# Batch 0's heads loaded together at the start, and its token weights converted behind its softmax

## The chip, the cores and the metric

The kernel runs on one NeuronCore of one Trainium2 chip. The metric is device time in microseconds (us) of one execution. Five engines run side by side, each through its own queue in order: TensorE (PE in the profile; PEld is its weight load), VectorE (DVE), ScalarE (ACT), GpSimd (POOL), and SyncE (SP), which here issues all DMAs.

## The reference

Three layers run one after the other on 4 batches of 576 positions and 512 features: a windowed attention with 8 heads, a phase-mixing layer, and a gated layer. All is float32; the weight matrices come in as float64.

```python
scores = where(mask, q @ k.T / sqrt(64), -1e9)          # window 32; heads 4..7 dilated by 4
x = softmax(scores) @ v                                  # -> (4, 576, 512)
theta = x @ w_theta
y = w_tok_r @ (x * cos(theta)) + w_tok_i @ (x * sin(theta))
u = x + y
x = u + relu(u @ w_ch)
h = relu(x @ w_in); u, v = halves(h)
out = (u * (w_spatial @ layernorm(v) + b_spatial)) @ w_out
```

## The kernel before, in words

Float32 products are made of three matmuls on rounded parts: each operand is split into a high part (`_h`) and the rest (`_l`), and high x high, low x high, high x low are summed in PSUM. Every float64 weight therefore goes through a conversion first (`split_weight`, which calls `bits64`): a DMA brings 256 or 288 columns as 64-bit words into a staging buffer `w` (tag w64, three of them); POOL or ACT scales the high words (L129 or L127, output `w64g`); DVE glues the low bits on in three instructions (L130, L131, L132, called a **triple** below); then the high part is copied out (L108 on ACT, L110 on DVE, L112 on POOL) and the low part subtracted (L143). For theta (`wth_h`, `wth_l`, 8 pieces) all but the triple is on POOL. The token weights `wtok_h`, `wtok_l` are 9 row blocks in two column halves of 9 pieces each: **tok0** (scale and high part on ACT, low part on POOL) and **tok1** (scale and high part on POOL, low part on DVE). `w_ch` has 8 pieces.

The stages of batch 0 are: attention, in 12 groups (4 head pairs hp, 3 groups g each): scores `s` (L220) and masks (L213) on PE, the maximum on DVE (L227), three exponentials on ACT (L235), sum and reciprocal on DVE (L236, L237), the product on POOL (L238), transposes (`pt`, L247), a copy (`pT`, L249), values (`ps_x`, L261 and L265) and copies to `x` (L268 to L277). Then theta in five units (`th_unit`): DVE splits x (`xh`, `xl`, L316, L317), PE forms `ps_th` (L322), ACT and DVE make sine and cosine, and `zh`, `zl` come out (L110, L112, L297). Then the token mixing `tm_run`: `ps_y` (L377) takes 9 row blocks times 3 matmuls for each of 8 outputs, added to x on DVE (L380). Then `ch_run` (`ps_r`, L395) with `w_ch`. Batch 1's attention is woven into the mixing of batch 0 and so on.

A call of `spread(main, (fill, rate), ...)` writes the program in the order main step, then `rate` steps of each fill. A scheduler then orders each engine's queue from that, and the queues run in that order on the chip: an instruction that waits holds all behind it on its engine. `tc.issue_after(i)` puts what is written under it behind instruction i in i's own queue. Buffers: head pairs alternate between two places for q (`qzero`), k and v, so head pair 2 can be loaded only when head pair 0's scores are done.

Of the kernel before, what the change touches and what calls it, by code (L numbers as in the profile page):

```python
# [2 lines left out]

# [19 lines left out]
DM = H * D  # L23
# [16 lines left out]


LAG_T, LAG_V = 2, 4
W_RATE0 = 0.75
ATT_RATE, ATT_RATE_PAIR = 2.0, 3.0
TAIL_RATE = 1.0
CH_BEFORE = 4
# [15 lines left out]
def tile_block(ctx: ExitStack, tc: tile.TileContext, qT, kT, vw, eye_in, mask_in, eye_b_in, w_theta, w_tok, w_ch, w_in, w_sp, w_sph, b_sp, w_out, out):  # L62
# [43 lines left out]
    def copy(dst, src, eng):  # L106
# [4 lines left out]
        else:  # L111
            G.tensor_scalar(dst, src, 1.0, 1.0, op0=ALU.mult, op1=ALU.mult)  # L112

    def bits64(src, n, eng):

        p = src.shape[0]
        st = const.tile([P, 2 * CH], U32, tag="w64", name="w64", bufs=3)
        SY.dma_start(st[:p, :2 * n], src.bitcast(U32))  # L120
        w = st[:p, :2 * n].rearrange("p (n w) -> p n w", w=2)
        lw, hw = w[:, :, 0], w[:, :, 1]
        g = const.tile([P, CH], F32, tag="stage", name="w64g", bufs=4)[:p, :n]
        c = c64[:p, :n].bitcast(U32)
        gi = g.bitcast(U32)
        if eng == "a":
            A.mul(g, hw.bitcast(F32), 2.0**-112)  # L127
        else:
            G.tensor_scalar(g, hw.bitcast(F32), 2.0**-56, 2.0**-56, op0=ALU.mult, op1=ALU.mult)  # L129
        V.tensor_scalar(c, lw, 29, None, op0=ALU.logical_shift_right)  # L130
        V.scalar_tensor_tensor(c, gi, 3, c, op0=ALU.logical_shift_left, op1=ALU.bitwise_or)  # L131
        V.scalar_tensor_tensor(gi, gi, 0x80000000, c, op0=ALU.bitwise_and, op1=ALU.bitwise_or)  # L132
        return g
# [27 lines left out]
    def w_tok_job(k, c):  # L161
        cs = slice(CH * c, CH * (c + 1))
        split_weight(w_tok[:, k, cs], wtok_h[:, k, cs], wtok_l[:, k, cs], *TOK_ENG[c])

    def w_ch_job(k):
        halves(w_ch, wch_h, wch_l, k, DM, CH_ENG)


    x = {}
# [3 lines left out]
    for i, qz in enumerate(qzero):  # L173
        for j in range(2):
            (V, G)[j].memset(qz[D * (1 - j):D * (2 - j), j], 0.0)

    groups = [(b, hp, g) for b in range(B) for hp in range(4) for g in range(3)]
    att = {}
    heads = {}

    def att_load(b, hp):
        qz = qzero[(4 * b + hp) % 2]
        kt = patt.tile([P, S + WIN], F32, tag="k", name="kt", bufs=2)
        first = b == 0 and hp == 0
# [12 lines left out]
        SY.dma_start(vt, vw[b, hp])
        heads[b, hp] = (qz, kt, vt, {})

    def att_scores(m):  # L200

        b, hp, g = groups[m]
        if g == 0:
            att_load(b, hp)
        if hp == 0 and g == 0:
            x[b] = p1.tile([P, 4, S], F32, tag="x", name=f"x{b}", bufs=2)
        qz, kt, vt, pT = heads[b, hp]
        s = ps_mm.tile([P, 512], F32, tag="mm", name="s")
# [12 lines left out]
        mask_half(False)
        sm = patt.tile([P, 3, KW], F32, tag="sm", name="sm", bufs=5)
        m_ = patt.tile([P, 3], F32, tag="m", name="m", bufs=3)
        l = patt.tile([P, 3], F32, tag="l", name="l", bufs=3)
        sv = s[:, :3 * KW].rearrange("p (t k) -> p t k", t=3)
        if on_pe:
            V.tensor_reduce(m_, sv, op=ALU.max, axis=AX.X, negate=True)  # L227
            A.mul(m_, m_, D**-0.5)
            src, scale = sv, D**-0.5
        else:  # L230
            V.scalar_tensor_tensor(sm, sv, D**-0.5, masks[:, kind], op0=ALU.mult, op1=ALU.add)  # L231
            V.tensor_reduce(m_, sm, op=ALU.max, axis=AX.X, negate=True)  # L232
            src, scale = sm, 1.0
        for t in range(3):
            A.activation(sm[:, t, :], src[:, t, :], AF.Exp, bias=m_[:, t:t + 1], scale=scale, accum_out=l[:, t:t + 1])  # L235
        V.tensor_scalar_add(l, l, 1e-9)  # L236
        V.reciprocal(l, l)  # L237
        G.tensor_tensor(sm, sm, l.unsqueeze(2).to_broadcast([P, 3, KW]), op=ALU.mult)  # L238
        att[m] = sm

    def att_transpose(m):
# [117 lines left out]
    def th_run(b, ts):  # L359
        for t in ts:  # L360
            th_unit(b, t)
            yield

    def tm_run(b, ks, last=True):

        if last:
            uh = p1.tile([P, 4, S], F32R, tag="uh", name="uh")
            ul = p1.tile([P, 4, S], F32R, tag="ul", name="ul")
            uu[b] = (uh, ul)
        for c in range(2):  # L370
            cs = slice(CH * c, CH * (c + 1))
            for d in range(4):
                ps = ps_mm.tile([P, 512], F32, tag="mm", name="ps_y")
                n = 0
                for k in ks:
                    for lh, rh in ((zh, wtok_h), (zl, wtok_h), (zh, wtok_l)):
                        PE.matmul(ps[:, :CH], lh[b, k][:, P * d:P * (d + 1)], rh[:, k, cs], start=(n == 0), stop=(n == 3 * len(ks) - 1))  # L377
                        n += 1
# [63 lines left out]
    j_out = [lambda k=k, c=c: stored(w_out, wo_d, k, slice(H2 * c, H2 * (c + 1)), OUT_ENG) for k in range(4) for c in range(2)]  # L442

    second = jobs(j_in + j_sp + j_out)
    spread(attention(0), (jobs(j_theta + j_tok0), W_RATE0))
    spread(th_run(0, (4, 0, 1, 2, 3)), (jobs(j_tok1), 1.0))
    for b in range(PAIR):
        ch = ch_run(b)
        spread(chain(tm_run(b, K_ALL), take(ch, CH_BEFORE)), (attention(b + 1), ATT_RATE), (take(second, 12) if b else jobs(j_ch), 1.0 if b else 0.5))
        run(th_run(b + 1, (4, 0, 1, 2, 3) if b + 1 < PAIR else (0, 1, 2, 3)))  # L450
        run(ch)

# [300 lines left out]
```

## Time and profile before

| | |
|---|---|
| runs | 575.29, 578.91 and 1181.34 us; median 578.91 |
| profiled execution | 575.99 us, of which the profile's span is 574.2 us |
| PE busy | 538.3 us (94% of the span) |
| DVE, ACT, POOL busy | 329.7, 243.3, 259.6 us |
| PE granted clock | 0.97 of full in the mean; below 0.9 only in some slices of the first 80 us and one later |

Engine shares are means over stages; the change lies in the first quarter of the span, so stretches of that quarter have to be read by themselves. Times in rows are microseconds from the span's start unless marked ns.

### The profile page before, as it was taken

To read this page: it belongs to the slowest core of one execution; us is meant where nothing else is said; L and a number is where in the kernel's file an instruction comes from. 1 tells how busy PE (TensorE), PEld (TensorE's weight loads), DVE (VectorE), ACT (ScalarE), POOL (GpSimd) and SP (SyncE) were. 2 spreads that over 40 slices of the span, in tenths; PEclk is the share of its full clock that TensorE was granted. 3 is DMA by queue.
4 is the path that set the end of the run, shared out by engine and by line. 5 is a ranking of instruction groups with operands and counts; after the bars stand their busy time and mean duration, and the time that the engine had idled before them with its cause. 6 is when DMAs were issued, how large, how long until landed. Compare 5 with 4: busy or idle time off the path is not lost.

```text
span 574.2 us, 11260 instructions
## 1 busy us (share of the span) xinstructions
PE 538.3 (94%) x4148; PEld 479.7 (84%) x4148; DVE 329.7 (57%) x842; ACT 243.3 (42%) x712; POOL 259.6 (45%) x329
## 2 busy tenths in 40 slices
PE   4958889999999999999799999999999999999997
PEld 2745668888988798888688999899889989988996
DVE  3767999965888548956688215773620227354030
ACT  3765475644465624677365111442332223233222
POOL 2755577633696436955339633343211303432040
PEclk9877989999999999999799999999999999999999
DMA  8996224762157644486510699805024120001002
GB/s 226 232 254 176 75 88 113 208 190 83 43 158 231 180 121 153 144 261 211 186 31 1 217 374 373 287 13 166 0 75 132 52 74 1 0 2 57 18 1 92
DMA packets 49935, 76.07 MB, mean 132 GB/s; under 512 B 4052, under 2 KB 30552, under 8 KB 49880
## 3 DMA queue, kind: packets, MB, share of 16 engines
q1 hardware_dynamic: 49880, 75.35, 42.9%
q8 instruction: 33, 0.54, 0.4%
q14 instruction: 22, 0.18, 0.1%
HBM read 52.53 MB, written 22.81 MB: 131 GB/s over the span
## 4 chain that ended last, share of the span: by engine, by line
PE 60%; DVE 13%; DMA 12%; POOL 5%; issue 4%; ACT 3%; SPq 1%; POOLq 0%; ACTq 0%; DVEq 0%
PE ps_y L377 10%; PE ps_sp L628 9%; PE ps_hu L609 9%; PE ps_o L657 9%; PE ps_hv L564 9%; PE ps_r L395 6%; DMA w<-w_tok 3%; PE s L220 2%; DMA w<-w_in 2%; DMA wsp_d<-parts 2%; PE ps_th L322 2%; POOL zl L297 2%; PE pt L247 1%; DMA qz<-qT 1%; DMA w<-w_ch 1%
## 5 line engine op out<-in xcount | busy, mean ns | idle before, releaser
L377 PE MATMUL ps_y<-wtok_h,zh 128*128 128x288 f32 x288 | 87.1, 308 | 3.3 <-DVE sm L231 1.3
L377 PE MATMUL ps_y<-wtok_h,zl 128*128 128x288 f32 x288 | 86.8, 303 | 2.4 <-POOL zl L297 2.4
L377 PE MATMUL ps_y<-wtok_l,zh 128*128 128x288 f32 x288 | 85.3, 297 | 0.0
L377 PEld LDWEIGHTS ps_y<-wtok_h,zh 128*128 128x128 f32 x288 | 53.9, 190 | 7.3 <-DVE sm L231 2.0
L297 POOL TENSOR_TENSOR gl<-hu,gh 128x288 fp32r<-128x288 f32 x32 | 26.0, 813 | 74.4 <-ACT gh L108 74.4
L377 PEld LDWEIGHTS ps_y<-wtok_h,zl 128*128 128x128 f32 x288 | 54.8, 190 | 4.4 <-POOL zl L297 3.2
L377 PEld LDWEIGHTS ps_y<-wtok_l,zh 128*128 128x128 f32 x288 | 54.7, 190 | 0.0
L632 DVE TENSOR_TENSOR hu<-ps_sp,hu 128x288 f32<-128x288 f32 x32 | 14.6, 456 | 67.0 <-PE ps_sp L631 66.9
L297 POOL TENSOR_TENSOR vl<-hv,vh 128x512 fp32r<-128x512 f32 x16 | 20.9, 1309 | 62.7 <-ACT vh L108 57.6
L235 ACT ACTIVATE sm<-sm,m 128x96 f32<-128x96 f32 x108 | 39.2, 364 | 14.6 <-DVE m L232 13.2
L220 PE MATMUL s<-kt,qz 128*64 128x96 f32 x576 | 42.3, 270 | 1.3 <-DMA qz<-qT 0.5
L220 PEld LDWEIGHTS s<-kt,qz 128*64 128x64 f32 x576 | 31.2, 147 | 11.1 <-issue 6.4
L238 POOL TENSOR_TENSOR sm<-sm,l 128x288 f32<-128x288 f32 x48 | 32.1, 673 | 18.1 <-DVE l L237 15.1
L297 POOL TENSOR_TENSOR ul<-x,uh 128x288 fp32r<-128x288 f32 x32 | 26.3, 830 | 27.3 <-ACT uh L108 27.2
L380 DVE TENSOR_TENSOR x<-ps_y,x 128x288 f32<-128x288 f32 x40 | 17.7, 449 | 35.5 <-PE ps_y L377 35.5
L395 PE MATMUL ps_r<-uh,wch_h 128*128 128x288 f32 x128 | 37.8, 296 | 0.0
L628 PE MATMUL ps_sp<-wsp_h,vh 128*128 128x288 f32 x128 | 37.8, 295 | 0.0
L297 POOL TENSOR_TENSOR parts<-x,parts 128x288 fp32r<-128x288 f32 x32 | 26.4, 831 | 25.3 <-ACT parts L108 25.3
L628 PE MATMUL ps_sp<-wsp_l,vh 128*128 128x288 f32 x128 | 37.8, 295 | 0.0
L628 PE MATMUL ps_sp<-wsp_h,vl 128*128 128x288 f32 x128 | 37.8, 295 | 0.0
L609 PE MATMUL ps_hu<-x2h,win_h 128*128 128x288 f32 x128 | 37.7, 294 | 0.0
L609 PE MATMUL ps_hu<-x2h,win_l 128*128 128x288 f32 x128 | 37.7, 294 | 0.0
(157 smaller groups left out, 1589.0 us busy)
## 6 DMA issues: line engine op xcount, KB each, us to landing
x2d<-parts SPq DMA_DIRECT2D x32, 288.0 KB, 2.4
vt<-vw SPq DMA_DIRECT2D x16, 432.0 KB, 4.5
w<-w_tok SPq DMA_DIRECT2D x18, 288.0 KB, 3.2
qz<-qT SPq DMA_DIRECT2D x32, 144.0 KB, 4.3
x2h<-x2d SPq DMA_DIRECT2D x8, 576.0 KB, 7.3
x2l<-x2d SPq DMA_DIRECT2D x8, 576.0 KB, 10.5
kt<-kT SPq DMA_DIRECT2D x15, 304.0 KB, 4.6
w<-w_in SPq DMA_DIRECT2D x16, 256.0 KB, 3.7
```

The lines of the kernel that those rows point to most:

```text
L220: PE.matmul(o, qz[:, j, T * t:T * (t + 1)], kt[:, T * t:T * t + KW], start=not on_pe, stop=not on_pe)
L235: A.activation(sm[:, t, :], src[:, t, :], AF.Exp, bias=m_[:, t:t + 1], scale=scale, accum_out=l[:, t:t + 1])
L238: G.tensor_tensor(sm, sm, l.unsqueeze(2).to_broadcast([P, 3, KW]), op=ALU.mult)
L297: (G if el == "g" else V).tensor_tensor(dst_l, src, f32(dst_h), op=ALU.subtract)
L377: PE.matmul(ps[:, :CH], lh[b, k][:, P * d:P * (d + 1)], rh[:, k, cs], start=(n == 0), stop=(n == 3 * len(ks) - 1))
L380: V.tensor_tensor(xv, ps[:, :CH], xv, op=ALU.add)
L395: PE.matmul(ps[:, :CH], lh[:, k, P * e:P * (e + 1)], rh[:, k, cs], start=(n == 0), stop=(n == 11))
L564: PE.matmul(ps, lh[:, k, ts_], rh[:, k, DM:], start=(n == 0), stop=(n == 11))
L609: PE.matmul(ps[:, :CH], lh[:, k, fs], rh[:, k, cs], start=(n == 0), stop=(n == 11))
L628: PE.matmul(ps[:, :CH], lh[b, k][:, fs], rh[:, k, cs], start=(n == 0), stop=False)
L632: V.tensor_tensor(t[:, f, cs], ps[:, :CH], t[:, f, cs], op=ALU.mult)
L657: PE.matmul(ps, lh[:, k, ts_], rh[:, k, cs], start=(n == 0), stop=(n == 11))
```

## The change

Head pairs 2 and 3 of batch 0 get places of their own for q, k and v, in memory that later holds `uh`, `ul`, `wch_h`, `wch_l`; so all four head pairs of batch 0 are loaded when its first group is written. The theta pieces follow behind these loads. The tok0 pieces are written beside theta, not beside attention, and each of their ACT, DVE and POOL instructions stands behind batch 0's last softmax instruction on that engine. The tok1 pieces move from beside theta to within the mixing, ahead of `w_ch`. The staging buffers become four. Batch 1's first two head pairs are loaded behind the last tok0 load. In the mixing of batch 0 the first two outputs are accumulated side by side, row block by row block.

```diff
-W_RATE0 = 0.75
+W_RATE0 = 0.5
+TOK_RATE = 2.25
...
-    wch_h = p1.tile([P, 4, DM], F32R, name="wch_h")
-    wch_l = p1.tile([P, 4, DM], F32R, name="wch_l")
...
+    last_dma = [None]
+
     def bits64(src, n, eng):
...
-        st = const.tile([P, 2 * CH], U32, tag="w64", name="w64", bufs=3)
-        SY.dma_start(st[:p, :2 * n], src.bitcast(U32))
+        st = const.tile([P, 2 * CH], U32, tag="w64", name="w64", bufs=4)
+        last_dma[0] = SY.dma_start(st[:p, :2 * n], src.bitcast(U32))
...
+    kt_2 = p1.tile([P, 2, S + WIN], F32, tag="ul", name="kt_2")
+    vt_2 = p1.tile([P, 2, NT, P], F32, tag="uh", name="vt_2")
+    qz_2 = [p1.tile([P, 2, S], F32, tag=n, name=f"qz_2{n}") for n in ("wch_h", "wch_l")]
+    for qz in qz_2:
+        for j in range(2):
+            G.memset(qz[D * (1 - j):D * (2 - j), j], 0.0)
...
     def att_load(b, hp):
-        qz = qzero[(4 * b + hp) % 2]
-        kt = patt.tile([P, S + WIN], F32, tag="k", name="kt", bufs=2)
+        early = b == 0 and hp >= 2
+        qz = qz_2[hp - 2] if early else qzero[hp % 2]
+        kt = kt_2[:, hp - 2] if early else patt.tile([P, S + WIN], F32, tag="k", name="kt", bufs=2)
...
-        if g == 0:
-            att_load(b, hp)
+        if g == 0 and (b or not hp):
+
+            with tc.issue_after(tok0_dma[-1].ins) if b == 1 and hp < 2 else nullcontext():
+                for h in range(1 if b else 4):
+                    att_load(b, hp + h)
...
+        last_softmax[b] = (ia, iv, ig)
...
+            early = b == 0 and c == 0
+            accs = []
             for d in range(4):
...
+                if early and d < 2:
+                    if d == 0:
+                        accs = [ps_mm.tile([P, 512], F32, tag="mm", name="ps_y") for _ in range(2)]
+                        for i, k in enumerate(ks):
+                            for e in range(2):
+                                for j, (lh, rh) in enumerate(((zh, wtok_h), (zl, wtok_h), (zh, wtok_l))):
+                                    PE.matmul(accs[e][:, :CH], lh[b, k][:, P * e:P * (e + 1)], rh[:, k, cs], start=(i + j == 0), stop=(i == len(ks) - 1 and j == 2))
+                    ps = accs[d]
...
-    spread(attention(0), (jobs(j_theta + j_tok0), W_RATE0))
-    spread(th_run(0, (4, 0, 1, 2, 3)), (jobs(j_tok1), 1.0))
+    def behind(f):
+
+        with ExitStack() as st:
+            for i in last_softmax[0]:
+                st.enter_context(tc.issue_after(i.ins))
+            f()
+        tok0_dma.append(last_dma[0])
+
+    spread(attention(0), (jobs(j_theta), W_RATE0))
+    spread(th_run(0, (4, 0, 1, 2, 3)), (jobs([lambda f=f: behind(f) for f in j_tok0]), 2.0))
     for b in range(PAIR):
         ch = ch_run(b)
-        spread(chain(tm_run(b, K_ALL), take(ch, CH_BEFORE)), (attention(b + 1), ATT_RATE), (take(second, 12) if b else jobs(j_ch), 1.0 if b else 0.5))
+        spread(chain(tm_run(b, K_ALL), take(ch, CH_BEFORE)), (attention(b + 1), ATT_RATE), (take(second, 12) if b else jobs(j_tok1 + j_ch), 1.0 if b else TOK_RATE))
```

On ACT, around the end of batch 0's attention, before (`w_519` and the like are staging buffers with token weights):

```order
L235 ACTIVATE sm,l<-s,m 128x96 x2
L127 ACTIVATE w64g<-w_430 128x288
L235 ACTIVATE sm,l<-s,m 128x96
L268 COPY x_118<-ps_x 128x192
L249 COPY pT<-pt 96x384
L228 ACTIVATE m<-m 128x3
L249 COPY pT<-pt 96x384
L108 CAST wtok_h<-w64g 128x288
L127 ACTIVATE w64g<-w_519 128x288
L235 ACTIVATE sm,l<-s,m 128x96 x3
L108 CAST wtok_h<-w64g 128x288
L273 COPY x_118<-ps_x 128x2x144
```

and now:

```order
L253 ACTIVATE sm,l<-s,m 128x96 x3
L292 COPY x_138<-ps_x 128x2x144
L293 COPY x_138<-ps_x 128x96
L268 COPY pT<-pt 96x384
L295 COPY x_138<-ps_x 128x48
L296 COPY x_138<-ps_x 128x144
L268 COPY pT<-pt 96x384 x2
L292 COPY x_138<-ps_x 128x2x144
L293 COPY x_138<-ps_x 128x96
L295 COPY x_138<-ps_x 128x48
L296 COPY x_138<-ps_x 128x144
L128 ACTIVATE w64g<-w_651 128x288
```

The scalings `w64g` and high parts `wtok_h` stood between the exponentials and copies of the last three groups; now the first of them stands behind the last copy to x.

On POOL, early in batch 0's attention, before:

```order
L129 TENSOR_SCALAR w64g<-w_159 128x256
L129 TENSOR_SCALAR w64g<-w_168 128x256
L238 TENSOR_TENSOR sm<-sm,l 128x288
L129 TENSOR_SCALAR w64g<-w_203 128x256
L112 TENSOR_SCALAR wth_h<-w64g 128x256
L143 TENSOR_TENSOR wth_l<-w64g,wth_h 128x256
L112 TENSOR_SCALAR wth_h<-w64g 128x256
L238 TENSOR_TENSOR sm<-sm,l 128x288
L129 TENSOR_SCALAR w64g<-w_212 128x256
L143 TENSOR_TENSOR wth_l<-w64g,wth_h 128x256
```

and now:

```order
L256 TENSOR_TENSOR sm<-sm,l 128x288 x6
L130 TENSOR_SCALAR w64g<-w_179 128x256
L130 TENSOR_SCALAR w64g<-w_188 128x256
L256 TENSOR_TENSOR sm<-sm,l 128x288
L130 TENSOR_SCALAR w64g<-w_249 128x256
L111 TENSOR_SCALAR wth_h<-w64g 128x256
L130 TENSOR_SCALAR w64g<-w_258 128x256
L256 TENSOR_TENSOR sm<-sm,l 128x288
L144 TENSOR_TENSOR wth_l<-w64g,wth_h 128x256
L111 TENSOR_SCALAR wth_h<-w64g 128x256
L256 TENSOR_TENSOR sm<-sm,l 128x288
```

Theta's first piece stood ahead of the first softmax product; now six products stand ahead of it, and the other six are woven in with the first pieces of theta.

On DVE, where x of batch 0 is complete (the first `xh`), before:

```order
L130 TENSOR_SCALAR c_101<-w_634 128x288
L131 SCALAR_TENSOR_TENSOR c_101<-w64g,c_101 128x288
L132 SCALAR_TENSOR_TENSOR w64g<-w64g,c_101 128x288
L130 TENSOR_SCALAR c_101<-w_658 128x288
L131 SCALAR_TENSOR_TENSOR c_101<-w64g,c_101 128x288
L316 TENSOR_SCALAR xh<-x_118 128x4x64
L316 TENSOR_SCALAR xh<-x_118 128x512
L132 SCALAR_TENSOR_TENSOR w64g<-w64g,c_101 128x288
L317 SCALAR_TENSOR_TENSOR xl<-x_118,xh 128x4x64
L317 SCALAR_TENSOR_TENSOR xl<-x_118,xh 128x512
L130 TENSOR_SCALAR c_101<-w_676 128x288
L131 SCALAR_TENSOR_TENSOR c_101<-w64g,c_101 128x288
```

and now:

```order
L132 SCALAR_TENSOR_TENSOR c_99<-w64g,c_99 128x256
L133 SCALAR_TENSOR_TENSOR w64g<-w64g,c_99 128x256
L131 TENSOR_SCALAR c_99<-w_420 128x256
L335 TENSOR_SCALAR xh<-x_138 128x4x64
L335 TENSOR_SCALAR xh<-x_138 128x512
L132 SCALAR_TENSOR_TENSOR c_99<-w64g,c_99 128x256
L336 SCALAR_TENSOR_TENSOR xl<-x_138,xh 128x4x64
L336 SCALAR_TENSOR_TENSOR xl<-x_138,xh 128x512
L133 SCALAR_TENSOR_TENSOR w64g<-w64g,c_99 128x256
L131 TENSOR_SCALAR c_99<-w_651 128x288
L132 SCALAR_TENSOR_TENSOR c_99<-w64g,c_99 128x288
L133 SCALAR_TENSOR_TENSOR w64g<-w64g,c_99 128x288
```

Before, six and two thirds of tok0's triples stood ahead of `xh`; now none does, tok0's nine triples all follow it, and theta's last piece is still under way there.

## Rows read from the trace of the kernel before

**Rows 1.** Busy time by stage: length, PE, PEld, DVE, ACT, POOL, clock, DMA share, GB/s.
```profile
0.00:48.10 48.10, 32.32 (x354) 22.55 (x354) 27.81 (x84) 28.45 (x123) 25.05 (x48) 0.81 0.93 237
...
66.40:90.20 23.80, 18.24 (x149) 14.53 (x147) 23.80 (x52) 15.76 (x42) 17.42 (x21) 0.93 0.25 73
90.20:124.80 34.60, 33.32 (x362) 30.03 (x362) 29.84 (x93) 20.06 (x77) 20.61 (x32) 1.00 0.72 199
124.80:132.60 7.80, 7.80 (x84) 7.54 (x83) 3.18 (x8) 2.48 (x7) 2.37 (x3) 1.00 0.31 99
```

**Rows 2.** Waits of ACT, 20 to 50 us: total us, times, longest.
```profile
ACT w64g L127 <- DMA w<-w_tok: 6.1, 6, 2.1
```

**Rows 3.** Chain of waits, 24 to 50 us: start, length, what.
```profile
31.55 7.44 DMA w<-w_tok
```

**Rows 4.** DVE timeline: first xh, last zh, two token instructions, w_ch's last high part.
```profile
48.14 0.91 DVE L316 TENSOR_SCALAR xh<-x 128x256 fp32r<-128x256 f32 x2 [1.16 <-ACT x L277]
...
87.76 1.05 DVE L110 CAST zh<-tb 128x512 fp32r<-128x512 f32 x1
...
91.77 0.45 DVE L130 TENSOR_SCALAR c<-w 128x288 uint32<-128x288 uint32 x1
92.13 0.44 DVE L143 TENSOR_TENSOR wtok_l<-w64g,wtok_h 128x288 fp32r<-128x288 f32 x1
...
113.01 0.72 DVE L110 CAST wch_h<-w64g 128x256 fp32r<-128x256 f32 x1
```

**Rows 5.** PE timeline: a mixing matmul; values, transposes and scores of one group; ch_run's first.
```profile
90.22 0.40 PE L377 MATMUL ps_y<-wtok_h,zl 128*128 128x288 f32 x1 [0.17 <-POOL zl L297]
...
98.12 0.57 PE L265 MATMUL ps_x<-pT,vt 96*64 96x64 f32 x12 [0.46 <-ACT pT L249]
98.62 0.53 PE L247 MATMUL pt<-ident,sm 128*96 128x128 f32 x3
99.09 0.72 PE L220 MATMUL s<-kt,qz 128*64 128x96 f32 x12
...
124.83 0.40 PE L395 MATMUL ps_r<-uh,wch_h 128*128 128x288 f32 x1
```

**Rows 6.** Chain of waits, 0 to 24 us.
```profile
6.87 7.25 DMA qz<-qT
```

**Rows 7.** DMA issues, 0 to 130 us: count, KB each, median us to landing.
```profile
vt<-vw SPq DMA_DIRECT2D x10, 432.0 KB, 4.7
qz<-qT SPq DMA_DIRECT2D x20, 144.0 KB, 6.3
kt<-kT SPq DMA_DIRECT2D x9, 304.0 KB, 6.9
w<-w_theta SPq DMA_DIRECT2D x8, 256.0 KB, 6.4
```

**Rows 8.** Groups of POOL instructions by shape, 0 to 130 us: busy, mean ns, idle before.
```profile
L238 POOL TENSOR_TENSOR sm<-sm,l 128x288 f32<-128x288 f32 x24 | 16.2, 678 | 7.1 <-DVE l L237 5.9 <-ACT w64g L127 0.9
...
L143 POOL TENSOR_TENSOR wth_l<-w64g,wth_h 128x256 fp32r<-128x256 f32 x8 | 5.8, 727 | 0.1
...
L129 POOL TENSOR_SCALAR w64g<-w 128x256 f32<-128x256 f32 x12 | 5.0, 421 | 15.4 <-DMA w<-w_theta 10.5 <-DMA w<-w_in 4.9
...
L112 POOL TENSOR_SCALAR wth_h<-w64g 128x256 fp32r<-128x256 f32 x8 | 3.3, 407 | 1.8 <-DVE l L237 1.8
...
L143 POOL TENSOR_TENSOR wtok_l<-w64g,wtok_h 128x288 fp32r<-128x288 f32 x9 | 7.3, 821 | 8.4 <-ACT wtok_h L108 8.4
```

**Rows 9.** ACT timeline: a pT copy and a copy to x.
```profile
44.28 0.47 ACT L249 COPY pT<-pt 96x384 f32<-96x384 f32 x1
...
46.31 0.65 ACT L273 COPY x<-ps_x 128x288 f32<-128x288 f32 x1
```

**Rows 10.** DVE timeline in theta of batch 1: the same instruction twice.
```profile
138.81 0.43 DVE L316 TENSOR_SCALAR xh<-x 128x512 fp32r<-128x512 f32 x1 [1.02 <-PE ps_th L322]
...
142.45 1.11 DVE L316 TENSOR_SCALAR xh<-x 128x512 fp32r<-128x512 f32 x1 [1.20 <-PE ps_th L322]
```

More of the change, by code (lines that the diff above doesn't have):

```diff
@@ L1 @@
 import math
-from contextlib import ExitStack
+from contextlib import ExitStack, nullcontext
 import ml_dtypes
@@ L163, in w_tok_job @@
         split_weight(w_tok[:, k, cs], wtok_h[:, k, cs], wtok_l[:, k, cs], *TOK_ENG[c])
+    wch = []
     def w_ch_job(k):
-        halves(w_ch, wch_h, wch_l, k, DM, CH_ENG)
+        if not wch:
+            wch.extend(p1.tile([P, 4, DM], F32R, tag=n, name=n) for n in ("wch_h", "wch_l"))
+        halves(w_ch, *wch, k, DM, CH_ENG)
     x = {}
@@ L175, in tile_block @@
             (V, G)[j].memset(qz[D * (1 - j):D * (2 - j), j], 0.0)
+    kt_2 = p1.tile([P, 2, S + WIN], F32, tag="ul", name="kt_2")
[4 more added lines that the diff above has]
+            G.memset(qz[D * (1 - j):D * (2 - j), j], 0.0)
+    last_softmax = {}
+    tok0_dma = []
     groups = [(b, hp, g) for b in range(B) for hp in range(4) for g in range(3)]
@@ L234, in att_scores @@
         for t in range(3):
-            A.activation(sm[:, t, :], src[:, t, :], AF.Exp, bias=m_[:, t:t + 1], scale=scale, accum_out=l[:, t:t + 1])
+            ia = A.activation(sm[:, t, :], src[:, t, :], AF.Exp, bias=m_[:, t:t + 1], scale=scale, accum_out=l[:, t:t + 1])
         V.tensor_scalar_add(l, l, 1e-9)
-        V.reciprocal(l, l)
-        G.tensor_tensor(sm, sm, l.unsqueeze(2).to_broadcast([P, 3, KW]), op=ALU.mult)
+        iv = V.reciprocal(l, l)
+        ig = G.tensor_tensor(sm, sm, l.unsqueeze(2).to_broadcast([P, 3, KW]), op=ALU.mult)
+        last_softmax[b] = (ia, iv, ig)
         att[m] = sm
@@ L362, in th_run, with u_tiles @@
             yield
+    def u_tiles(b):
+        if b not in uu:
+            uu[b] = tuple(p1.tile([P, 4, S], F32R, tag=n, name=n) for n in ("uh", "ul"))
+        return uu[b]
     def tm_run(b, ks, last=True):
         if last:
-            uh = p1.tile([P, 4, S], F32R, tag="uh", name="uh")
-            ul = p1.tile([P, 4, S], F32R, tag="ul", name="ul")
-            uu[b] = (uh, ul)
+            uh, ul = u_tiles(b)
         for c in range(2):
             cs = slice(CH * c, CH * (c + 1))
+            early = b == 0 and c == 0
+            accs = []
             for d in range(4):
[L373 to L378, printed above, removed]
+                if early and d < 2:
[6 more added lines that the diff above has]
+                    ps = accs[d]
+                else:
+                    ps = ps_mm.tile([P, 512], F32, tag="mm", name="ps_y")
+                    n = 0
+                    for k in ks:
+                        for lh, rh in ((zh, wtok_h), (zl, wtok_h), (zh, wtok_l)):
+                            PE.matmul(ps[:, :CH], lh[b, k][:, P * d:P * (d + 1)], rh[:, k, cs], start=(n == 0), stop=(n == 3 * len(ks) - 1))
+                            n += 1
                 xv = x[b][:, d, cs]
@@ L387, in ch_run @@
         uh, ul = uu.pop(b)
+        wch_h, wch_l = wch
         for c in range(2):
```

2 lines of the change are left out of this document (1 added, 1 removed).

## The prediction

> **What bounds the kernel now.** I read four views. The stage table first [rows 1]: the columns after the length are the busy times of PE, its weight load, DVE, ACT and POOL. From 90.2 us on PE is the bound: 33.3 of 34.6 us, then 7.8 of 7.8. Before that it is not. In the first 48.1 us PE is busy for 32.3 at a mean granted clock of 0.81, a mixture of the 1.2 and 2.4 GHz levels, and no engine is full; DMA is (0.93, 237 GB/s). From 66.4 to 90.2 DVE is busy without a gap and PE for 18.2 of 23.8. So a gain must come out of the first 90 us, and it counts only as far as PE can start its later work sooner.
>
> Second, the waits of ACT [rows 2] and the chain [rows 3] tell what holds the first stage: ACT waits six times, 6.1 us, for token weights whose scaling stands in its queue ahead of softmax exponentials and copies to x; one such load is 7.4 us of the chain. Batch 0's x is complete only when the first xh starts, at 48.14 [rows 4]. Third, the DVE timeline [rows 4]: from there to the end of the last zh (87.76 + 1.05 = 88.8) DVE needs 40.7 us, and to the end of the last high part of w_ch (113.01 + 0.72 = 113.7) another 24.9. Fourth, PE [rows 5]: the first mixing matmul behind the last of the zl is at 90.2, ch_run begins at 124.8. I follow these four marks (x, last zh, PE's 90.2, ch_run) through the change; behind ch_run the orders are nearly alike and PE is full, so its shift is the gain.
>
> **Step 1, x is ready earlier.** One head pair is 304 + 2 x 144 + 432 = 1024 KB [rows 7]. At 14.1 us (6.87 + 7.25) [rows 6] head pair 0, three theta pieces and k and q of head pair 1 had landed: 1024 + 768 + 592 = 2384 KB. If the same bytes are head pairs alone, 4096 - 2384 = 1712 KB (1.75 MB) are left, 7.4 us at 237 GB/s [rows 1]: all heads are in at 21.5, theta's first 256 KB at 22.6. That is a delay for theta's conversion, which is mostly POOL's. POOL's order now has six products ahead of theta; from 22.6 to the last softmax product it holds 6 products, 6 scalings, 4 high and 3 low parts: 6 x 0.678 + 6 x 0.421 + 4 x 0.407 + 3 x 0.727 = 10.4 us [rows 8], so 33.0. From there x takes a transpose (0.53) and values (0.57) [rows 5], a pT copy (0.47) and four copies to x, of which the longest takes 0.65 [rows 9]; with the small ones I estimate 1.1 for the four and 0.6 for the hand-overs: 3.3 together. x is complete at 36.3, 11.8 us earlier. Bounds: 30 if POOL is not what holds it (heads at 21.5, three groups of exponentials and the tail), 40 if the rows of POOL find their inputs late. I take 36.3, since in the rows before POOL ran its theta rows nearly without idle (0.1 us ahead of the low parts).
>
> **Step 2, the last zh.** Between the first xh and the last zh DVE's order holds seven token triple instructions of 288 or 256 columns more and five low parts fewer, one mask addition, one pT copy and two small softmax instructions fewer. Two neighbours in the timeline start 0.36 apart [rows 4]; the balance is 2 x 0.36 - 0.36 - 0.5 - 0.4 = -0.5. Tok0's triples come in and tok1's go out, so nothing is saved here. 36.3 + 40.7 - 0.5 = 76.5 (12.3 earlier), and PE goes on at 77.9.
>
> Here a port matters. The same xh takes 0.43 us in one place and 1.11 in another [rows 10], and the 0.82 us low parts of tok0 [rows 8] move from beside attention to beside theta. By its order POOL has seven low parts more in this stretch, four scalings, five high parts and a product fewer, which is about even, so I charge nothing; the upper bound is 9 x 0.82 = 7.4. The Trainium skill (page "SBUF — State Buffer", section "Who interferes with whom") says that VectorE and GpSimd share a port pair, held for a whole instruction by whoever came first; the two durations agree with it, and by it alone up to those 7.4 us would be added and x's gain mostly lost.
>
> **Step 3, PE up to ch_run.** Behind the last zl PE has the same 153 mixing matmuls as before, and more of batch 1's attention: 6 score matmuls (0.72), one set of transposes (0.53), 11 value matmuls (about 1.0) [rows 5]: 34.6 + 2.2 = 36.8. That would be 114.7 for ch_run, 10.1 earlier.
>
> **Step 4, DVE up to the last w_ch.** The tok1 conversions that stood beside theta now stand here: 15 triple instructions, 5 low parts, 5 of softmax and 2 additions to x more, 27 x 0.36 = 9.7; with 6 small ones and a copy (1.5) it is 24.9 + 11.2 = 36.1, so 112.6, and POOL's last low part 0.73 later [rows 8]: 113.3. DVE and PE then end within 1.4 us of each other, both full for 37 us, and each waits for the other (maxima and additions on DVE, scores and sums on PE). What that costs no row shows. Lower bound 0: in the stretch before, PE lost 1.3 of 34.6 with DVE at 86%, which is in the sum already. Upper bound 8.7: while DVE was full PE lost 5.6 of 23.8 [rows 1], times 36.8. I take 2.0, nearer the first, because here all z are ready and only the token weights come piece by piece. ch_run starts at 116.7, **8.1 us earlier**.
>
> **The rest.** Thirteen triple instructions of w_in pass behind w_ch's, about 4.4 us of DVE; they fall into ch_run, where DVE is busy for 3.2 of 7.8 us [rows 1]: no cost, at most 4.4 if that cover is gone. The four memsets come before POOL's first product: nothing. The two outputs accumulated side by side are the same matmuls. On SP the four loads of batch 1 wait behind the last tok0 load, which needs a staging buffer that DVE frees about 13 us behind x; their first scores stand some 10 us later still in DVE's and PE's order: nothing. Later the clock is taken as it was.
>
> Sum: 575.99 - 8.1 = **567.9 us**, against the profiled execution's own time, which lies 0.5% below the median of the runs shown (578.91) and 0.1% above the lowest (575.29).
>
> **Rivals.** *Full shift.* No mutual waiting, and x at 33: 575.99 - 10.1 - 3.3 = 562.6. For it: 90.2 to 124.8, where PE lost little beside a DVE at 86%. Against it: DVE has no slack at all. Chance 0.20 (below 564.5).
>
> *The port takes it back.* Tok0's nine low parts, now beside theta's casts, hold DVE up: with all 7.4 us 575.3, with half 571.6. For it: the two durations [rows 10]. Against it: POOL's load in that stretch does not grow. The skill's page named above is the rule behind it. Chance 0.20 (572 to 577).
>
> *Slower: w_ch's loads come late.* On SP most of the w_ch loads now stand behind reloads of k, q and v that wait for PE's scores or values, at four places. A triple that waits for its load holds maxima and additions behind it on DVE, and PE waits for these, which delays the next reload. Each time costs up to a landing, 4.7 to 6.9 us [rows 7]. By the steps above PE frees those places 5 to 9 us ahead of the triples; it decides from the point where that lead is below the landing time. Two full waits give -8.1 + 2 x 4.7 = +1.3, 577; four give 586.7. Chance 0.13 (577 to 587), about a third of it above 587.5 with the other costs added.
>
> The forecast (564.5 to 572, with x between 33 and 40 and 0 to 5 us of mutual waiting) has 0.47.
>
> **How the numbers follow.** The predicted time is the forecast's. The range 560 to 577.5 leaves out the slower case and the far end of the full shift, 0.18 in all. Two per cent is about what a measurement of this kernel can tell from no change; against 575.99 that is 564.5 and 587.5. Faster by more: the full shift, 0.20, and 0.05 from the forecast's edge, since the median may lie a little above the profiled time: 0.25. Slower by more: 0.04. Within: 0.71.
>
> **What would show it.** Step 1: no wait of ACT for token weights before batch 0's x, first xh at 33 to 40, heads landed by 22. Step 2: the last zh ends 40 us behind the first xh; if 45, the port did it, and the casts are longer. Steps 3 and 4: ch_run's first matmul at 114 to 119, DVE without gaps from x to there, and w_ch ending within 3 us of it; a wait of DVE for w_ch's load there is the slower rival. If PE has gaps behind ch_run that were not there before, the shift is given back later, which no step of mine contains.

## The result and the profile after

The changed kernel takes **569.9 us** (median of four runs, 569.3 to 572.5) against 576.3 for the kernel before in the same comparison (median of three, 575.3 to 578.9): a ratio of 0.989, with a 95% interval of 0.985 to 0.994. One run of before, 1181.34 us, took twice as long as the others and is left out here, while the median of 578.91 given ahead of the prediction still counts it. The forecast was 567.9, within 2%, in the range 560 to 577.5. The profiled execution takes 569.31 us, its span 567.5 (before: 575.99 and 574.2): 6.7 us less, where 8.1 were forecast.

The four marks of the prediction, in us:

| mark | before | forecast | after |
|---|---|---|---|
| first xh starts (x is ready) | 48.1 | 36.3 | 38.1 |
| last zh ends | 88.8 | 76.5 | 80.7 |
| PE goes on behind the last zl | 90.2 | 77.9 | 82.5 |
| ch_run's first matmul | 124.8 | 116.7 | 118.2 |

The stage table of after, with the columns of [rows 1]: length, busy time of PE, its weight load, DVE, ACT and POOL, granted clock, DMA share, GB/s.

```profile
0.00:38.10 38.10, 28.13 (x354) 20.44 (x354) 20.72 (x66) 22.15 (x106) 21.00 (x43) 0.91 0.75 199
58.50:82.50 24.00, 17.08 (x145) 14.50 (x144) 21.45 (x50) 15.08 (x41) 19.91 (x24) 0.86 0.49 130
82.50:118.10 35.60, 35.60 (x391) 32.06 (x387) 33.58 (x100) 21.04 (x82) 22.85 (x37) 1.00 0.68 195
118.10:126.00 7.90, 7.90 (x69) 7.33 (x66) 7.40 (x19) 2.47 (x7) 5.43 (x8) 1.00 0.59 165
```

The first stage is 10.0 us shorter, its DMA share has fallen from 0.93 to 0.75, and the stage up to ch_run has PE busy throughout. Behind the start of ch_run the kernels take 449.4 and 449.3 us (574.2 - 124.8, 567.5 - 118.2): the shift of 6.6 is kept whole. The marks in the timelines of DVE and then PE, after, answering to [rows 4] and [rows 5]:

```profile
38.13 0.72 DVE L335 TENSOR_SCALAR xh<-x 128x256 fp32r<-128x256 f32 x2 [0.81 <-ACT x L296]
...
80.29 0.41 DVE L109 CAST zh<-tb 128x512 fp32r<-128x512 f32 x1
...
118.81 0.29 DVE L109 CAST wch_h<-w64g 128x256 fp32r<-128x256 f32 x1
```

```profile
82.52 0.40 PE L404 MATMUL ps_y<-wtok_h,zl 128*128 128x288 f32 x1
...
118.19 0.40 PE L430 MATMUL ps_r<-uh,wch_h 128*128 128x288 f32 x1
```

The waits of ACT from 15 to 45 us in after (total, times, longest) hold one wait for a token weight, 1.2 us, behind the last copy to x, where [rows 2] had six and 6.1. What replaced them is the first row, DVE's maxima, which stand behind theta's first piece:

```profile
ACT m L246 <- DVE m L245: 3.3, 1, 3.3
...
ACT w64g L128 <- DMA w<-w_tok: 1.2, 1, 1.2
```

The chain of waits of after, 15 to 45 us, shows how long the heads and theta's first piece take; it landed at 23.5, forecast 22.6:

```profile
7.24 7.83 DMA kt<-kT
15.09 8.46 DMA w<-w_theta
```

POOL's last softmax product, in its timeline, ends at 34.4 (33.76 + 0.67), forecast 33.0:

```profile
33.76 0.67 POOL L256 TENSOR_TENSOR sm<-sm,l 128x288 f32<-128x288 f32 x1 [0.24 <-ACT pT L268]
```

One new wait stands between x and the last zh. SP's issues around 51 to 56 us, POOL's timeline and PE's, all of after:

```profile
51.57 0.42 SPq L202 DMA_DIRECT2D kt<-kT  x1
...
54.30 0.47 SPq L204 DMA_DIRECT2D qz<-qT  x1
56.06 0.33 SPq L121 DMA_DIRECT2D w<-w_tok  x1
```

```profile
61.86 0.44 POOL L130 TENSOR_SCALAR w64g<-w 128x288 f32<-128x288 f32 x1 [2.10 <-DMA w<-w_tok]
62.27 0.94 POOL L111 TENSOR_SCALAR zh<-ta 128x512 fp32r<-128x512 f32 x1
63.29 1.26 POOL L316 TENSOR_TENSOR zl<-ta,zh 128x512 fp32r<-128x512 f32 x1
64.51 1.26 POOL L316 TENSOR_TENSOR zl<-tb,zh 128x512 fp32r<-128x512 f32 x1
```

```profile
65.83 0.61 PE L404 MATMUL ps_y<-wtok_h,zl 128*128 128x288 f32 x1 [4.41 <-POOL zl L316]
```

The second token half's first piece is issued at 56.06, behind six loads of batch 1's heads. POOL waits 2.10 us for it, and behind its scaling in POOL's order stand the zh and zl that PE wants; PE stands for 4.41.

### The profile page after: what moved, and what is told of

Read it like the earlier page. It is cut to its first block, busy times and chain, and to the rows that moved or that the text cites. A ratio compares the mean times of both kernels' runs of the same rounds, so it can differ in the third digit from the quotient of the medians.

```text
span 567.5 us, 11263 instructions
## 1 busy us (share of the span) xinstructions
PE 534.8 (94%) x4148; PEld 478.4 (84%) x4148; DVE 331.0 (58%) x844; ACT 241.9 (43%) x710; POOL 262.1 (46%) x333
## 4 chain that ended last, share of the span: by engine, by line
PE 62%; DVE 10%; DMA 9%; POOL 7%; ACT 5%; issue 5%; SPq 1%; POOLq 0%; DVEq 0%; ACTq 0%
PE ps_y L411 12%; PE ps_sp L671 9%; PE ps_hu L652 9%; PE ps_o L700 9%; PE ps_hv L607 9%; PE ps_r L430 6%; POOL zl L316 2%; DMA wsp_d<-parts 2%; PE ps_th L341 2%; DMA w<-w_theta 1%; PE s L238 1%; DMA kt<-kT 1%; PE pt L266 1%; DVE xl L336 1%; DMA x2d<-parts 1%
## 5 line engine op out<-in xcount | busy, mean ns | idle before, releaser
L411 PE MATMUL ps_y<-wtok_h,zh 128*128 128x288 f32 x270 | 81.8, 306 | 1.7 <-DVE ta L346 0.9
L411 PE MATMUL ps_y<-wtok_h,zl 128*128 128x288 f32 x270 | 81.1, 301 | 0.4 <-POOL zl L316 0.4
L411 PE MATMUL ps_y<-wtok_l,zh 128*128 128x288 f32 x270 | 80.0, 298 | 0.0
L411 PEld LDWEIGHTS ps_y<-wtok_h,zh 128*128 128x128 f32 x270 | 50.7, 189 | 4.9 <-DVE sm L249 1.3
L411 PEld LDWEIGHTS ps_y<-wtok_h,zl 128*128 128x128 f32 x270 | 51.0, 189 | 1.9 <-POOL zl L316 0.8
L411 PEld LDWEIGHTS ps_y<-wtok_l,zh 128*128 128x128 f32 x270 | 50.8, 189 | 0.2
L652 PE MATMUL ps_hu<-x2l,win_h 128*128 128x288 f32 x128 | 37.7, 295 | 0.0
L652 PE MATMUL ps_hu<-x2h,win_h 128*128 128x288 f32 x128 | 37.7, 295 | 0.0
L652 PE MATMUL ps_hu<-x2h,win_l 128*128 128x288 f32 x128 | 37.7, 295 | 0.0
L430 PE MATMUL ps_r<-uh,wch_l 128*128 128x288 f32 x128 | 37.7, 296 | 0.0
L430 PE MATMUL ps_r<-ul,wch_h 128*128 128x288 f32 x128 | 37.4, 295 | 0.0
## 6 DMA issues: line engine op xcount, KB each, us to landing
x2h<-x2d SPq DMA_DIRECT2D x8, 576.0 KB, 7.7
x2l<-x2d SPq DMA_DIRECT2D x8, 576.0 KB, 10.9
```

What stands on the lines that cost most here:

```text
L430: PE.matmul(ps[:, :CH], lh[:, k, P * e:P * (e + 1)], rh[:, k, cs], start=(n == 0), stop=(n == 11))
L652: PE.matmul(ps[:, :CH], lh[:, k, fs], rh[:, k, cs], start=(n == 0), stop=(n == 11))
```

## The experiments

The first theory was the prediction's: token pieces in ACT's and DVE's order within batch 0's attention held x, and taking them out made the gain. Where an edit changes the program's order, the scheduler lays all orders anew, so every run is read by the same marks. Here, by DVE's timeline, "token pieces" counts DVE's first instruction of each piece of the token weights up to the first xh.

| run | time, us | ratio (95%) | token pieces before x | first xh | last zl ends | ch_run |
|---|---|---|---|---|---|---|
| before | 576.3 | | 7 | 48.1 | 90.2 | 124.8 |
| after | 569.9 | 0.989 (0.985-0.994) | 0 | 38.1 | 82.3 | 118.2 |
| e1 | 569.3 | 0.988 (0.986-0.990) | 0 | 38.0 | 82.7 | 120.2 |
| e2 | 568.6 | 0.987 (0.985-0.989) | 4 | 39.4 | 83.5 | 117.8 |
| e3 | 567.3 | 0.983 (0.980-0.987) | 0 | 38.4 | 81.2 | 118.7 |
| e4 | 568.7 | 0.988 (0.984-0.992) | 0 | 39.2 | 88.3 | 122.2 |
| e6 | 570.4 | 0.988 (0.984-0.992) | 0 | 38.1 | 82.8 | 120.3 |
| e7 | 572.8 | 0.991 (0.988-0.994) | 5 | 45.7 | 86.7 | 122.2 |
| e8 | 569.0 | 0.986 (0.981-0.990) | 5 | 39.9 | 82.5 | 119.1 |
| e9 | 565.7 | 0.980 (0.976-0.984) | 5 | 40.0 | 85.2 | 117.0 |
| e10 | 571.6 | 0.990 (0.986-0.994) | 0 | 40.8 | 84.1 | 120.1 |
| e11 | 573.1 | 0.994 (0.991-0.997) | 7 | 42.6 | 91.9 | 126.6 |
| e12 | 565.6 | 0.980 (0.975-0.986) | 5 | 40.1 | 85.6 | 117.4 |
| f1 | 568.4 | 0.985 (0.982-0.989) | 0 | 39.6 | 82.6 | 118.5 |

Ratios are to the kernel before in the same comparison. The median of before was 575.9 beside e1 to e4, 577.8 beside e6 to e8, 576.9 beside e9 to e11 and f1, and 574.8 beside e12, so runs of different comparisons are set against each other by their ratios. The times are medians, while the marks come from the one profiled execution of each run.

How far the marks move without any change of the order can be read from e1 and e6: by their timelines, the orders of DVE, ACT, POOL and SP up to ch_run are those of after (see below), and yet ch_run begins at 120.2 and 120.3 instead of 118.2. For the same zh near 80 us PE waits 1.05 us in after and 1.39 in e1 and e6. In after the granted clock then stays at 1.00, in e1 and e6 it is at the 1.2 GHz level (0.50) from 84 to 86 us. The stage rows of these 2 us, of after and then of e1:

```profile
84.00:86.00 2.00, 2.00 (x17) 2.00 (x17) 2.00 (x6) 1.20 (x8) 1.55 (x3) 1.00 0.87 318
```

```profile
84.00:86.00 2.00, 2.00 (x10) 2.00 (x9) 2.00 (x6) 1.19 (x8) 1.96 (x4) 0.50 0.91 297
```

So a difference in ch_run of some 2 us decides nothing here.

### First: undo one part at a time (e1 to e4)

e1 puts the first token half back beside the attention:

```
-W_RATE0 = 0.5
+W_RATE0 = 0.75
...
-    spread(attention(0), (jobs(j_theta), W_RATE0))
-    spread(th_run(0, ...), (jobs([lambda f=f: behind(f) for f in j_tok0]), 2.0))
+    spread(attention(0), (jobs(j_theta + j_tok0), W_RATE0))
+    tok0_dma.append(last_dma[0])
+    run(th_run(0, ...))
```

> The changed kernel with its first token half (nine pieces) put back between the attention steps of batch 0; heads at once, second half in the mixing and the side by side sums stay. Theory (the token pieces' waits in ACT and DVE held the attention): the first xh comes at 45 to 48 us again instead of 38.1; theta then has nothing beside it, so the last zh at 82 to 85 instead of 80.7; the time 571 to 575 us instead of 569.9. Rival (the heads loaded at once made the gain): the first xh stays at 37 to 40, and the time is 567 to 570.

Measured: first xh at 38.0. But the scheduler itself put every token piece behind the attention in ACT's order, as in after, since their loads come behind the four heads and theta. So e1 did not undo what it was meant to undo, and decides nothing on the theory; it is a second measurement of after's order, and shows that the explicit hold of the conversions is not needed once the heads come first.

e2 loads the heads one after another again (`early = False`, `att_load` at each head's first group).

> The changed kernel with the heads loaded one after another into the two shared buffers, as before the change; the token halves stay where the change put them. Theory: without token pieces in front of them the heads' loads come in time, the first xh stays at 37 to 40 us and the time at 569 to 571.5. Rival (heads): the first xh comes at 44 to 48, the time is 574 to 577.

Measured: first xh at 39.4, 568.6 us. Loading the heads at once is not needed either. Either of two parts alone seemed to be enough.

e3 issues one load earlier:

```
+    tok1_jobs = jobs(j_tok1 + j_ch)
+    next(tok1_jobs)
+    tok0_dma.append(last_dma[0])
...
```

> The changed kernel with one load moved: the first piece of the second token half is issued ahead of batch 1's first two heads instead of behind six of their loads. On PE, DVE and POOL nothing changes its place. Theory (POOL's wait of 2.1 us for that piece near 60 us holds the zh and zl casts queued behind it, and DVE and PE behind those): that wait is gone, the last zh ends at 78 to 79.3 instead of 80.7, the time is 567.5 to 568.8. Rival (the wait only hides DVE's own load): the last zh stays within 0.5 of 80.7 and the time within 569 to 571.

Measured: POOL's wait of 2.1 for that load is gone, PE's longest wait for a zl falls from 4.4 to 1.8, and the last zh ends at 79.7: 1.0 earlier, half of what the theory gave, twice what the rival allowed. From the first xh on, which came 0.2 later, it is 1.3. At ch_run, which begins at 118.7 instead of 118.2, nothing of it is left to see. The four runs spread from 564.1 to 570.5, and the interval overlaps that of after: at most a small gain.

e4 computes the mixing's first two sums one after the other.

> The changed kernel with the mixing's first two sums computed one after the other, as before the change, instead of side by side. Theory: the token pieces are converted before the mixing needs them, so the pairing matters little: the stretch from the last zl to ch_run stays within 1 us of 35.7 and the time within 569 to 571. Rival (the pairing covers late pieces of zh or of the token weights): PE waits more at the mixing's start and the time is 572 to 575.

Measured: from the last zl to ch_run 33.8 us instead of 35.9, but theta's stretch grew and ch_run came 4.0 later. The median, 568.7, is that of after; the profiled execution, on which the marks rest, was the slowest of the four, 572.1. Neither reading is borne out as a whole.

### Second: what is left when both parts are undone (e6 to e8)

e8 joins the edits of e1 and e2; five token pieces now really stand before x.

> The changed kernel with both the heads' loads and the first token half put back as before the change (e1 and e2 together); kept are the fourth staging buffer, the second token half in the mixing and the side by side sums. Unlike in e1, seven token pieces now stand ahead of batch 0's last x copy in ACT's order. Theory (token pieces within the attention hold x, and either of e1's and e2's edits alone keeps them out of it): the first xh comes at 44 to 49 us instead of 38.1, the last zl ends at 86 to 90, the time is 572 to 576 instead of 569.9. Rival (the second token half in the mixing or the fourth buffer made the gain): the first xh may come later, but the time stays at 568 to 570.5.

Measured: first xh at **39.9**. The first theory falls: token pieces stand within the attention again and x is nearly as early as in after. Time and ch_run are also those of after.

e7 is the kernel before with one edit, `name="w64", bufs=4`.

> The kernel before the change with a fourth staging buffer for the weights and nothing else. Six token pieces still stand ahead of batch 0's last x copy in ACT's order. Theory: the first xh comes at 44 to 48 us instead of 48.1 and the time is 573 to 577, against 575.9 before. Rival (the wait was for a free staging buffer, so the buffer alone makes the gain): the first xh at 38 to 41 and the time 567 to 571.

Measured: first xh at 45.7, a median of 572.8 us over nine runs (the profiled one, 576.0, was the slowest), 0.991 of before: by these medians the fourth buffer alone gives most of what the whole change gives, though the intervals overlap. The prediction had not priced it at all.

e6 gives the second token half back to theta's stretch in the program (`behind` tok0, then `+ j_tok1`, rate 4.0).

> The changed kernel with the second token half put back beside theta (behind the first), so that the mixing has only the channel weights beside it. Theory (what counts is when x is ready; the token work costs the engines as much beside theta as within the mixing): the first xh stays at 37 to 39.5, theta's stretch gets longer and the mixing's shorter by about as much, the time is 568.5 to 571. Rival (the second half in the mixing is part of the gain, because theta is bound by DVE and POOL while the mixing is bound by PE): the last zl ends at 86 to 90 and the time is 572.5 to 576.

Measured: the time of after, but DVE's timeline has the same 12 pieces beside theta and the same 6 behind the last zl as in after. The scheduler laid the work as in after, so this is a third measurement of the same order and says nothing on the theory.

### Third: why x is early in e8 and late in e7 (e9 to e11)

Both have five token pieces before x on DVE. What differs before x is SP's order. In e7 the heads of batch 1 are loaded among the token pieces; e8 has them behind the last of these, by the `issue_after(tok0_dma[-1].ins)` that the change also brings. e9 is e7 with that line and what it needs (`tok0_dma` is given the last load of tok0):

```
+            with tc.issue_after(tok0_dma[-1].ins) if b == 1 and hp < 2 else nullcontext():
+                att_load(b, hp)
```

> e7 (the kernel before with a fourth staging buffer) with one thing more: batch 1's first two heads' loads are issued only behind the last load of the first token half. Six token pieces stand ahead of batch 0's last x copy in ACT's order, in e7 as here. New theory, after e8 (what held x was not the place of the token pieces in ACT's order but that they landed late, with 2.0 MB of batch 1's heads in the DMA queue among them): the first xh comes at 39 to 42 us instead of e7's 45.7, the time is 569 to 571.5 instead of 572.8. Rival (the first theory: the token pieces in the attention's order hold x, and e8 was early for another reason): the first xh at 44 to 47, the time 572 to 574.

Measured: first xh at 40.0 (e7: 45.7), and **565.7 us**, 0.980 of before: faster than was expected, and faster than the whole change, whose interval (0.985 to 0.994) begins where e9's (0.976 to 0.984) ends. On ACT seven token scalings now stand ahead of batch 0's last copy to x, in e7 six: the place in the order got worse, and x came earlier. (The profiled executions, from which the marks come, took 576.0 us in e7, its slowest, and 566.3 in e9.) SP's issues in e7, among the token loads; then the chain of waits of e7:

```profile
24.69 0.47 SPq L189 DMA_DIRECT2D qz<-qT  x1
...
26.07 0.38 SPq L187 DMA_DIRECT2D kt<-kT  x1
26.57 0.35 SPq L120 DMA_DIRECT2D w<-w_tok  x1
26.97 0.50 SPq L193 DMA_DIRECT2D qz<-qT  x1
29.15 0.47 SPq L189 DMA_DIRECT2D qz<-qT  x1
29.73 0.53 SPq L120 DMA_DIRECT2D w<-w_tok  x1
30.35 0.38 SPq L187 DMA_DIRECT2D kt<-kT  x1
```

```profile
26.57 7.66 DMA w<-w_tok
...
34.30 9.71 DMA w<-w_tok
...
44.57 0.55 ACT x L273
```

Two token loads in a row make 17.4 of the 18 us up to the copy to x. SP's issues in e9, same stretch: five token loads, and only then batch 1's first.

```profile
32.21 7.11 SPq L123 DMA_DIRECT2D w<-w_tok  x5
39.37 1.51 SPq L190 DMA_DIRECT2D kt<-kT  x1
```

Transfers from 24 to 40 us (count, KB, median us from issue to landing) and the waits of ACT from 15 to 50 us, first of e7, then of e9:

```profile
ACT w64g L127 <- DMA w<-w_tok: 7.9, 7, 1.8
...
w<-w_tok SPq DMA_DIRECT2D x7, 288.0 KB, 8.6
```

```profile
ACT w64g L130 <- DMA w<-w_tok: 2.3, 1, 2.3
...
w<-w_tok SPq DMA_DIRECT2D x8, 288.0 KB, 3.5
```

The same 288 KB land in 3.5 instead of 8.6 us, and ACT's waits fall from 7.9 to 2.3; the 2.3 stand behind the last copy to x. The stage rows from 26.6 to 44 us, of e7 and then of e9, have the DMA share, the last figure but one, at 1.05 and at 0.71:

```profile
26.60:44.00 17.40, 11.54 (x170) 8.97 (x170) 11.38 (x36) 11.35 (x49) 9.04 (x16) 0.82 1.05 248
```

```profile
26.60:44.00 17.40, 15.19 (x195) 10.63 (x190) 16.46 (x48) 13.70 (x58) 11.32 (x18) 1.00 0.71 206
```

So it was not the place of the pieces in the engines' order that held x, but that they landed late, with the heads of batch 1 sharing the DMA, whose first scores PE starts in e7 only at 64.3.

e10 turns it round: after without that line. ACT's order up to x is that of after.

> The changed kernel without the rule that batch 1's first two heads are loaded behind the last load of the first token half: their eight loads (2.0 MB) now stand ahead of the theta weights' second half and of all token pieces in SP's queue. ACT's order does not change at all, and no token piece stands within the attention. New theory (the 2.0 MB come first, at the 230 to 250 GB/s of these loads some 8 us, estimated from the trace): theta's later pieces land late, POOL and DVE wait for them ahead of the last softmax, the first xh comes at 42 to 47 us instead of 38.1, the time is 571 to 576. Rival (the place of the token pieces in the order is what counts, and theta's pieces have room): the first xh at 37 to 39.5, and with the second token half loaded earlier the time is 567 to 570.

Measured: first xh at 40.8, between the two; the time of 571.6 is in the theory's band, but its interval overlaps that of after. The waits of POOL and DVE from 15 to 50 us in e10 show that the new late transfers are theta's:

```profile
POOL w64g L130 <- DMA w<-w_theta: 8.1, 6, 4.1
```

```profile
DVE c L131 <- DMA w<-w_theta: 6.4, 4, 2.9
```

The direction is the theory's, the size (2.7 us of x, not 4 to 9) is not: only six of the eight loads (both k and q, 1.2 MB) come ahead of theta's second half; the two v (0.9 MB) came between its pieces.

e11 is the kernel before with three buffers and that line alone.

> The kernel before the change, with its three staging buffers, and one thing changed: batch 1's first two heads' loads are issued behind the last load of the first token half. All nine token pieces now stand ahead of batch 0's last x copy in ACT's order (eight before). New theory: the first xh comes at 40 to 44 us instead of 48.1 (the three buffers still make the pieces wait for each other), the time is 570 to 574 against 576 to 578 before. Rival (first theory: the order within ACT): nine pieces ahead instead of eight, the first xh at 47 to 50, the time 576 to 579.

Measured: first xh at 42.6, as the new theory says, with eight token scalings on ACT and seven pieces on DVE ahead of x, as many as before (the expectation counted nine on ACT); but theta's stretch then takes 49.3 us instead of 42.0, and ch_run begins at 126.6, later than before. The median of ten runs, 573.1, is in the theory's band; the profiled run, on which the marks rest, was the slowest, 577.7. The waits of POOL from 42 to 127 us in e11, and from 40 to 117 in e9, point to where the lack of a fourth buffer is paid:

```profile
POOL w64g L132 <- DMA w<-w_tok: 12.1, 5, 3.8
```

```profile
POOL w64g L132 <- DMA w<-w_tok: 7.3, 3, 4.4
```

The two parts make a square: 0.991 for the buffer, 0.994 for the line, 0.980 for both. The two savings, 0.9% and 0.6%, make 1.5% of the 2.0%; the rest is within the intervals.

### Fourth: going on (f1, e12)

f1 relieves DVE in the mixing: `TOK_ENG = ("aga", "ag")` instead of `("aga", "gv")`.

> An attempt to go on: the changed kernel with the second token half's high parts on ACT instead of POOL and its low parts on POOL instead of DVE. Within the mixing DVE loses nine subtractions of 0.61 us, 5.5 us. Theory (DVE, busy 37.7 of 40 us there, sets when ch_run begins): ch_run begins at 113 to 116.5 us instead of 118.2 and the time is 565 to 568.5. Rival (PE with its matmuls is the bound behind the last zl, or POOL's and ACT's new work holds the softmax): ch_run at 117.5 to 120, the time 569 to 572.

Measured: ch_run at 118.5, as the rival said; the time, 568.4 us, lies at the edge of the theory's band, and its interval overlaps that of after. DVE had 36.4 instead of 37.7 us of work between 80 and 120, and ch_run did not come earlier for it. That fits the rival: PE was already busy for 35.6 of 35.6 us in that stretch of after.

e12 is e8 with the first two sums one after the other. In the program it then differs from e9 mainly by the second token half, in the mixing instead of beside theta; the change's four memsets and its places for `w_ch` stay too.

> e8 with the mixing's first two sums one after the other. Against e9 (565.7 us: the kernel before with the fourth buffer and batch 1's loads held behind the first token half) this kernel then differs by the second token half alone, which stands in the mixing instead of beside theta; e8 (569.0) has the pairing besides. In all three x is ready at 39.9 to 40 us, and the stretch from the first xh to ch_run was 77.1 us in e9 and 79.2 in e8. Theory (the token half moved into the mixing is what costs e8 its 3 us: DVE, the bound there, gets it later): that stretch stays at 78.5 to 80.5 us and the time at 568 to 570. Rival (the pairing costs it, since both sums wait for each late zh and zl): the stretch falls to 76 to 77.7, the time to 565 to 567.

Measured: 565.6 us, 0.980, the time of e9. The stages from the first xh to the last zl and on to ch_run, of e8 and then of e12:

```profile
39.90:82.50 42.60, 33.17 (x207) 25.87 (x209) 38.75 (x86) 22.34 (x51) 27.36 (x34) 0.90 0.51 140
82.50:119.00 36.50, 36.50 (x411) 33.95 (x409) 33.02 (x101) 22.36 (x83) 21.62 (x36) 0.93 0.69 195
```

```profile
40.10:85.60 45.50, 36.58 (x253) 29.59 (x254) 39.89 (x92) 27.33 (x62) 27.57 (x37) 0.89 0.54 144
85.60:117.40 31.80, 31.80 (x351) 28.87 (x349) 29.86 (x90) 19.99 (x73) 20.79 (x32) 1.00 0.64 184
```

But the second half did not move. The last token piece that DVE converts, in e9 and then in e12:

```profile
90.27 0.45 DVE L133 TENSOR_SCALAR c<-w 128x288 uint32<-128x288 uint32 x1
```

```profile
90.67 0.44 DVE L131 TENSOR_SCALAR c<-w 128x288 uint32<-128x288 uint32 x1
```

All eight pieces from 59.9 us on follow in e12 about 0.4 us behind their place in e9. Up to 120 us ACT's order is the same in both, and those of DVE, POOL and SP differ by one softmax instruction, the four memsets and one v load. So e12 does not test its theory: it measures e9's order once more and finds the same 0.980. As e1 and e6 (both 0.988) do so for after (0.989), three measurements of one order stand against two of the other, 0.8 to 0.9% apart. Against e8, unpaired, the last zl ends 3.1 us later, but with more of PE's work behind it (253 matmul records before it, 207 in e8), what follows has a granted clock of 1.00 instead of 0.93, and ch_run begins 1.7 earlier, which is no more than the marks move by themselves. By time alone e8 and e12 are not apart (their intervals overlap), and in e4 the same edit brought ch_run later, so the pairing's price is not settled. What of the change, then, makes it 0.9% slower than e9 also stays open: the pairing is a candidate, not shown. Of the 3.1 us between the two profiled spans (567.5 and 564.4) 1.2 lie ahead of ch_run and 1.9 behind it.

## Why the prediction was right, and where it was not

**Step 1, x.** 36.3 forecast, 38.1 measured, within the bounds. The mechanism of the sum holds: theta's first piece landed 0.9 later than worked out, POOL's part up to its last product took 10.9 us instead of 10.4, and the tail 3.7 instead of 3.3. DVE holding batch 0's maxima for theta's first piece (the 3.3 us of ACT) was not foreseen, but POOL's part grew by only 0.5. The reason given for the late x was half right. The rows showed token loads on the chain [rows 2, 3]; the step took their place in ACT's order for the fault. e8 and e9 show that pieces may stand there if they land in time, and the 0.93 of the DMA in [rows 1] was a hint that they shared it.

**"The rest: on SP the four loads of batch 1 wait behind the last tok0 load: nothing."** This is the step that failed, on both sides. Holding these loads is what frees the DMA for the token pieces (e9 against e7: 5.7 us of x; within the change, where theta's pieces are what it frees the DMA for, 2.7 us of x by e10, and no difference in time beyond the intervals); and as the change has it, they stand ahead of the second half's first piece, a wait of 2.1 us for POOL and part of 4.4 for PE. They were looked at for the wait of their own users alone, not for what shares the queue with them.

**The fourth staging buffer** is in the diff and in no term of the sum; alone it gives 0.991 (e7). No run has the change with three buffers, so what it is worth within the change is not shown.

**Step 2.** The last zh ends 42.6 us behind the first xh, forecast 40.2; the wait that e3 takes away explains 1.3 of the 2.4. The port, charged at nothing, came out even in this sense: the four zh casts on DVE took 0.41 to 0.54 us instead of 1.05 to 1.47, while xl, beside a zl and a low part of tok0 on POOL, took 1.58 once where it had taken 0.68. The 1.1 us that are left over are less than that rival's 3.7 to 7.4. The rule of the Trainium skill (page "SBUF — State Buffer", section "Who interferes with whom") would lay such differences to what POOL does at the same moment; no run here separates that.

**Steps 3 and 4.** From PE's mark to ch_run 35.7 us, forecast 36.8 + 2.0. PE had no gap there, so the 2.0 for mutual waiting was the mis-sized term; with 1.1 of the 36.8 it makes up for the 2.8 by which step 2 is late at PE's mark (44.4 us behind the first xh, forecast 41.6). DVE's part was too short: w_ch's last high part was to end at 112.6, 36.1 behind the last zh, and ends at 119.1, 38.4 behind it and 0.9 behind ch_run's start. It did not hold PE, and in f1 a lighter DVE moved nothing.

That ch_run came within 1.5 us of the forecast is in part luck: at PE's mark the sum was 4.6 us short, and 3.1 of them came back in a stretch that took less than was summed.

**The rivals.** No wait of DVE for w_ch's loads appears, so the slower case did not come. The full shift failed by x at 38.1 and by step 2.

## What to carry to other kernels

When an engine waits for a load that stands on the chain, look first at what else is in the queue and on the DMA at that time and when that is wanted, and hold back the loads with the latest use: one such line and one more staging buffer gave what the whole rearrangement gave, and more (0.980 against 0.989). An edit to a program that a scheduler lays out may be undone by the scheduler; read from the trace whether it took place before drawing anything from its time. A load that is moved has two prices, to those who wait for it and to those who share the queue with it.

## What the runs showed of the hardware that was not expected

After PE's wait of 4.41 us in after, its granted clock was at the 1.2 GHz level (0.50) for the next 5 us, and 26 matmuls were done where the following 4.2 us, at 0.99, saw 53:

```profile
61.40:65.80 4.40, 0.02 (x1) 0.00 (x0) 2.19 (x6) 1.01 (x2) 3.85 (x5) 0.80 0.74 184
65.80:70.80 5.00, 4.97 (x26) 4.47 (x27) 4.76 (x12) 2.50 (x5) 5.00 (x6) 0.50 0.23 62
70.80:75.00 4.20, 4.20 (x53) 3.68 (x52) 4.20 (x10) 4.14 (x10) 4.20 (x6) 0.99 0.29 84
```

So a wait of PE can cost over half as much again behind it: 5 us at half the clock are some 2.5 us of matmuls, an estimate from these rows. How much of that reached the last zl is not shown; DVE was busy for 21.45 of theta's last 24.0 us. In e1 and e6 the 2 us by which ch_run came later followed on such a stretch.
